# First weight tiles split by hand in halves, one weight tile per unit, and a new sharing of the second layer's split and clamp steps in an attention and two-MLP kernel

## The chip, the cores and the metric

The kernel runs on one core of a Trainium2 chip. The metric is the device time in microseconds (us), from launch to end. The engines are named as in the profile: PE (TensorE, matmuls), PEld (its weight loads), DVE (VectorE), ACT (ScalarE), POOL (GpSimd) and SP (SyncE, which issues DMAs).

## The reference

Banded attention with a slope per head is followed by two MLPs, all on 2304 tokens (4 x 576) of 512 features, 8 heads of 64:

```python
scores = scale * np.matmul(q, k.transpose(0, 1, 3, 2))
rel = pos[:, None] - pos[None, :]
mask = (rel >= 0) & (rel < 128)
scores = np.where(mask, scores + slope * -abs(rel), -1e9)
attn = softmax(scores)                 # over the keys
x = (attn @ v) as [2304, 512]
...
h = np.maximum(x @ w_in, 0.0);  x = h * h @ w_out      # d_ff = 2048
...
h = x @ w_in;  g = h * np.cos(h);  out = g @ w_out
```

## The kernel before, in words

Every matmul with float32 accuracy is done as three matmuls of split operands: each tile is split into a high part (`wh`, `xh`, `rh`/`gh`) that the PE takes as it is, and a low part (`wl`, `xl`, `rl`/`gl`), the rest. ACT makes the high parts (a cast), DVE the low ones (a subtraction).

**Attention.** A step is a pair of heads of 128 query rows, `s` = 4 j + hp. The first 16 steps go as eight pairs (`pairs`) and use "plain" tiles `S0`. For a pair, PE makes scores, DVE the row minima with the bias (`minima`, L666), ACT the exponentials (`exps`, L682), then the rows are scaled by one over their sum (`normalise`, L696 to L706), PE transposes them (L715), ACT copies the transposed tile out of PSUM (L717), POOL masks it with two selects (`transposes`, L722), and PE multiplies with v (`values`, L768). `x_hi` (L788) and `x_lo` (L791) split the result for layer 1. Throughout, `fill(n)` (L123) puts n matmuls on constant data into PE's order, where it would have nothing to do. The first eight pairs and the work up to the second score tile are written out in order by hand under `tc.manual_schedule`; from there a scheduler orders each engine's instructions by the order of the program and by its own estimates, and each engine runs them in that order.

**Layer 1.** `h_mms(i)` (L827 to L829) makes the h tile of a unit i (128 of the 2048 inner columns for 512 tokens), ACT and DVE make the square of its positive part, and `y_mms(i)` (L956 to L958) adds it to y. The raw weight tile `raw_f` of a unit holds both halves, w_in and w_out, and three steps split it: `w_top` (L241, ACT, a copy of the top 16 bits into a zeroed tile `cv`), `w_rest` (L245, DVE, the rest by shift and or), `w_split` (L258, ACT, the high part) and its late step `lo` (L261, DVE, the low part). Each works on 1024 columns. A `tick()` moves each job that is under way by one step and starts new ones ("a": keys and queries or block sums, "w": weights).

**Layer 2.** Its first product is done by seven products of half blocks (`seven`), so that sums of blocks (S1 to S4 of the weights, T1 to T4 of x) have to be formed and split beforehand, and products are put together by copies (L863, L864, L868, L876, ACT) and additions (L865, L871, L874, DVE) into `hs`. Units go in pairs p (`NP` of them), a pair in four quarters with one tick each. Jobs make the weights: `blocks_job(u)` (L348, L364 to L367) and `w2_job(u)` (L295), both with L241 and L245, `x2_sums_job` (L465 and others) the sums of x. `LATE` says at which pair the last two weight blocks may start, `LEAD` after how many ticks a loaded job may. A unit's activation is `cos_reduce` (ACT L905, DVE L906 and L907, a clamp to +-4.7 on DVE, L908, and the absolute value on ACT, L909) and `cos_apply` (the sine on ACT, L917, product on DVE L918, split by L919 and L920). `y_out` copies a block of y (L971) and stores it.

Of the kernel before, what the change touches and what calls it, by code (L numbers as in the profile page):

```python
# [31 lines left out]
INV2PI = 1.0 / (2.0 * math.pi)  # L32
C1 = 6.28125
# [24 lines left out]
START, PLAIN, FILLS = 16, 7, (19, 5, 10, 4, 14, 6)  # L58


A_OPEN, START_W, MERGED = 20, (5,), 16
# [10 lines left out]
NP = NBK * NU  # L72
RING = (2, 3, 4, 5)
# [5 lines left out]
class Job:  # L79


    def __init__(self, key, load, stages, gates=None, source=None, frees=1, ready=None, raws=1):
# [6 lines left out]
def attention_mlp_mlp(ctx: ExitStack, tc: tile.TileContext, kq, s0, v, w1, w2, bias, ident, out):  # L89
# [21 lines left out]
    warm = cst.tile([P, 1], F32, name="warm")  # L111
    dve.memset(halfpi, math.pi / 2)
    act.activation(warm, halfpi, AF.Exp)
# [23 lines left out]
    LATE = (2, 5), (3, 6)  # L137
# [82 lines left out]
    def w_load(layer, f):  # L220
        def load(job):
            job.raw = wp.tile([P, 2048], F32, tag=f"w{f}", name=f"raw_{layer}_{f}")
# [41 lines left out]

    def w_job(layer, f):
# [10 lines left out]
    def w2_job(u):  # L276
# [16 lines left out]
        def lo(job):  # L293
# [4 lines left out]
            ("w2", u), load, [w_top, w_rest, split, lo], {0: aged(u, 1)}, frees=2, ready=lambda: now["y"] >= used(u) and due(u, 1)  # L298
# [12 lines left out]
    def blocks_job(u):  # L311
# [66 lines left out]
        def end(job):  # L378
# [10 lines left out]
            ready=lambda: now["y"] >= used(u) and gp2 is not None and due(u, 0),  # L389
        )  # L390
# [56 lines left out]
    def x2_sums_job(b, k):  # L447
# [33 lines left out]
        def lo(job):  # L481
            for (dst, src), (top, _) in zip(views(job, 1), views(job, 0)):
                dve.tensor_tensor(dst, src, top.bitcast(F32), ALU.subtract)

# [5 lines left out]
        return Job(("x", b, k), load, [sums, hi, lo], {0: gate}, ("y", b), frees=2, raws=2)  # L490

    def x2_job(b, m):
# [6 lines left out]
        def lo(job):  # L499
# [8 lines left out]
            ("y", b),  # L508
        )
# [167 lines left out]
    def exps(steps):  # L677
# [12 lines left out]
        if len(steps) == 2:  # L690
            pool.tensor_scalar(st[:, 2], st[:, 1], 1e-9, None, ALU.add)

    def normalise(*steps):
        st = St.pop(steps)
        if len(steps) == 1:
# [12 lines left out]
    def transposes(*steps):  # L708
# [7 lines left out]
        quick = steps == pairs[-1]  # L716
# [570 lines left out]
```

## Time and profile before

| what | value |
|---|---|
| time, median of 3 runs (lowest to highest) | 903.06 us (902.13 to 904.57) |
| the profiled execution | 904.49 us |
| its span from first to last instruction | 902.8 us (1.7 us lie outside) |
| PE, DVE, ACT, POOL busy | 892.0, 639.4, 531.9, 104.6 us |
| mean granted TensorE clock | 0.998 of full |

The profile's rows come from one profiled execution, whose time stands above the median of the runs by 1.43 us. An engine's idle time counts only where it is on the way to the end; PE is busy for 99% of the span.

### The profile page before, as it was taken

To read this page: it belongs to the slowest core of one execution; us is meant where nothing else is said; L and a number is where in the kernel's file an instruction comes from. 1 tells how busy PE (TensorE), PEld (TensorE's weight loads), DVE (VectorE), ACT (ScalarE), POOL (GpSimd) and SP (SyncE) were. 2 spreads that over 40 slices of the span, in tenths; PEclk is the share of its full clock that TensorE was granted. 3 is DMA by queue.
4 is the path that set the end of the run, shared out by engine and by line. 5 is a ranking of instruction groups with operands and counts; after the bars stand their busy time and mean duration, and the time that the engine had idled before them with its cause. 6 is when DMAs were issued, how large, how long until landed. Compare 5 with 4: busy or idle time off the path is not lost.

```text
span 902.8 us, 15383 instructions
## 1 busy us (share of the span) xinstructions
PE 892.0 (99%) x5474; PEld 764.0 (85%) x5474; DVE 639.4 (71%) x1533; ACT 531.9 (59%) x1177; POOL 104.6 (12%) x164
## 2 busy tenths in 40 slices
PE   9899999999999999999999999999999999999998
PEld 7677788888888888788888889888988989899987
DVE  7699676656676556745776788998877776666654
ACT  6799555455454444524655686776666755655543
POOL 3333221102222112200100100000000000000000
PEclk9999999999999999999999999999999999999999
DMA  9852031311122111224899999977657655655530
GB/s 373 292 219 94 13 128 59 106 47 60 59 71 72 57 48 47 90 97 166 270 313 319 311 344 301 316 224 238 202 179 227 208 168 173 215 182 169 185 127 24
DMA packets 82141, 153.24 MB, mean 170 GB/s; under 512 B 7696, under 2 KB 29584, under 8 KB 82064
## 3 DMA queue, kind: packets, MB, share of 16 engines
q1 hardware_dynamic: 81632, 152.06, 51.0%
q8 instruction: 43, 0.70, 0.3%
q14 instruction: 34, 0.28, 0.1%
q10 hardware_dynamic: 432, 0.20, 0.1%
HBM read 126.01 MB, written 26.21 MB: 169 GB/s over the span
## 4 chain that ended last, share of the span: by engine, by line
PE 83%; DVE 8%; ACT 4%; DMA 3%; issue 1%; POOL 0%; SPq 0%; DVEq 0%; ACTq 0%; POOLq 0%
PE y L956 12%; PE y L957 12%; PE y L958 12%; PE h L827 7%; PE h L829 7%; PE h L828 7%; PE s L855 5%; PE s L857 5%; PE s L856 5%; PE o L768 3%; PE s L616 2%; PE t L715 1%; DVE cv_w L245 1%; DVE w L261 1%; DMA raw_a<-kq_in 1%
## 5 line engine op out<-in xcount | busy, mean ns | idle before, releaser
L956 PE MATMUL y<-rh,w 128*128 128x512 f32 (+1 forms) x320 | 120.9, 379 | 0.0
L827 PE MATMUL h<-xh,w 128*128 128x512 f32 (+1 forms) x320 | 119.7, 374 | 0.0
L957 PE MATMUL y<-rl,w 128*128 128x512 f32 (+1 forms) x320 | 118.6, 371 | 0.0
L958 PE MATMUL y<-rh,w 128*128 128x512 f32 (+1 forms) x320 | 118.5, 370 | 0.0
L828 PE MATMUL h<-xl,w 128*128 128x512 f32 (+1 forms) x320 | 118.1, 369 | 0.0
L829 PE MATMUL h<-xh,w 128*128 128x512 f32 (+1 forms) x320 | 118.0, 369 | 0.0
L956 PE MATMUL y<-gh,w 128*128 128x512 f32 x256 | 101.1, 395 | 0.0
L957 PE MATMUL y<-gl,w 128*128 128x512 f32 x256 | 101.0, 395 | 0.0
L958 PE MATMUL y<-gh,w 128*128 128x512 f32 x256 | 99.7, 389 | 0.0
L883 ACT ACTIVATE a<-h 128x512 f32<-128x512 f32 x72 | 42.9, 596 | 80.1 <-PE h L829 79.9
L722 POOL TENSOR_SCALAR_AFFINE_SELECT p<-p 128x256 f32<-128x256 f32 x104 | 61.6, 593 | 235.0 <-ACT p L717 231.5
L894 DVE TENSOR_TENSOR a<-a 128x512 f32<-128x512 f32 x62 | 43.9, 708 | 48.4 <-ACT rh L893 47.7
L682 ACT ACTIVATE p<-s,st 128x128 f32<-128x128 f32 x112 | 40.1, 363 | 60.2 <-DVE st L666 57.8
L855 PE MATMUL s<-xh,arena 128*128 128x256 f32 x256 | 73.0, 286 | 1.4 <-DVE hs L865 1.2
L857 PE MATMUL s<-xh,arena 128*128 128x256 f32 x256 | 72.4, 283 | 0.0
L856 PE MATMUL s<-xl,arena 128*128 128x256 f32 x256 | 72.3, 283 | 0.0
L827 PEld LDWEIGHTS h<-xh,w 128*128 128x128 f32 x320 | 60.4, 189 | 11.5 <-issue 0.5
L905 ACT ACTIVATE kk<-hs 128x512 int32<-128x512 f32 x64 | 39.6, 631 | 51.6 <-DVE hs L874 50.9
L958 PEld LDWEIGHTS y<-rh,w 128*128 128x128 f32 x320 | 60.3, 188 | 10.4
L829 PEld LDWEIGHTS h<-xh,w 128*128 128x128 f32 x320 | 60.3, 188 | 10.4
L956 PEld LDWEIGHTS y<-rh,w 128*128 128x128 f32 x320 | 60.4, 189 | 9.9 <-issue 1.7
L828 PEld LDWEIGHTS h<-xl,w 128*128 128x128 f32 x320 | 60.4, 189 | 9.3
(142 smaller groups left out, 2207.9 us busy)
## 6 DMA issues: line engine op xcount, KB each, us to landing
arena<-wd SPq DMA_DIRECT2D x256, 256.0 KB, 3.3
raw<-w_in SPq DMA_DIRECT2D x16, 1023.8 KB, 7.9
raw_a<-kq_in SPq DMA_DIRECT2D x44, 256.0 KB, 3.0
raw<-w_in SPq DMA_DIRECT2D x16, 511.8 KB, 7.0
raw_b<-w_in SPq DMA_DIRECT2D x16, 511.8 KB, 6.5
wd<-hi_b SPq DMA_DIRECT2D x10, 512.0 KB, 5.4
v<-v_in SPq DMA_DIRECT2D x18, 256.0 KB, 2.8
y<-ysb SPq DMA_DIRECT2D x18, 256.0 KB, 2.0
```

What stands on the lines that cost most here:

```text
L722: pool.affine_select(pt[:, part], pt[:, part if quick else 0], pattern=[[0, n], [0, 2], [-sign, P]], compare_op=ALU.is_gt if part else ALU ...
L827: te.matmul(o, wh, xh, start=(c == 0 and kt == 0), stop=False, skip_group_check=True)
L828: te.matmul(o, wh, xl, start=False, stop=False, skip_group_check=True)
L829: te.matmul(o, wl, xh, start=False, stop=(kt == KT - 1), skip_group_check=True)
L855: te.matmul(o, wh, xh, start=opens and k == 0, stop=False, skip_group_check=True)
L856: te.matmul(o, wh, xl, start=False, stop=False, skip_group_check=True)
L857: te.matmul(o, wl, xh, start=False, stop=k == 1, skip_group_check=True)
L883: act.activation(Aa[i], Hb.pop(i), AF.Relu)
L894: dve.tensor_tensor(a, a, a, ALU.mult)
L956: te.matmul(o, wh, gh, start=(first and not (two and m % 2)), stop=False, skip_group_check=True)
L957: te.matmul(o, wh, gl, start=False, stop=False, skip_group_check=True)
L958: te.matmul(o, wl, gh, start=False, stop=last, skip_group_check=True)
```

## The change

The core of it, by parts:

- The start: the first two weight tiles, w_0 and w_1, are split in halves of 512 columns each (`w_half_job`; first w_in, then w_out), in steps called by hand (`step`). Raw tiles 0 and 1 use other seats. The last pair is scaled by DVE alone; DVE also makes the small additions of the last two pairs and masks one part of each (`quick`) by a multiplication with `onward`. The fills are changed.
- Layer 1: a new weight job starts in the first tick of a unit, not in each.
- Layer 2: a tick starts at most one step of a job that is marked heavy on DVE (`fits`, `heavy`); the low part of the block sums of x is made in two steps; `LATE` and `LEAD` are lower; and for units NG1 + 6 to NG1 + 17 (pairs 3 to 8) ACT does the clamp.

```diff
-START, PLAIN, FILLS = 16, 7, (19, 5, 10, 4, 14, 6)
-A_OPEN, START_W, MERGED = 20, (5,), 16
+START, PLAIN, FILLS = 16, 7, (19, 5, 10, 4, 14, 4)
+BY_HAND = 2
+ACT_CLIPS = range(NG1 + 6, NG1 + 2 * NU + 2)
...
-    LATE = (2, 5), (3, 6)
+    LATE = (1, 3), (2, 5)
...
     def advance(job):
-        with behind() if timed(job) else ExitStack():
+        with behind() if timed(job) or job.key[0] in ("w", "kq") else ExitStack():
...
     def tick(new="aw", flush=True):
         ticks[0] += 1
+        worked = [0]
+        def fits(job):
+            if now["p"] < 0 or not timed(job) or not job.heavy[job.at]:
+                return True
+            worked[0] += 1
+            return worked[0] == 1
         for job in list(inflight):
-            if job.at not in job.gates or job.gates[job.at]():
+            if (job.at not in job.gates or job.gates[job.at]()) and fits(job):
...
-                if job.raw is None or timed(job) and ticks[0] < job.loaded + (LEAD if now["p"] < 0 else 2 * LEAD - 2):
+                if job.raw is None or timed(job) and ticks[0] < job.loaded + (LEAD + 3 if job.key[0] != "x" and job.key[1] > 5 else LEAD):
                     continue
-                if 0 not in job.gates or job.gates[0]():
+                if (0 not in job.gates or job.gates[0]()) and fits(job):
...
+    def w_half_job(layer, f):
+        def top(job, c):
+            if job.t is None:
+                job.t = cleared.pop(0)
+                w = wp.tile([P, 2048], F32R, tag=f"w{f}", name=f"w_{layer}_{f}")
+                W[layer, f] = (w[:, 0:512], w[:, 1024:1536]), (w[:, 512:1024], w[:, 1536:2048])
+            f16 = job.t.bitcast(F16).rearrange("p (c n two) -> p c n two", c=2, two=2)
+            raw = job.raw.bitcast(BF16).rearrange("p (c n q) -> p c n q", c=2, q=4)
+            act.copy(f16[:, c, :, 1], raw[:, c, :, 2])
+        def half(job, c):
+            return job.t[:, 512 * c : 512 * c + 512]
+        def rest(job, c):
+            raw = job.raw.bitcast(I32).rearrange("p (c n two) -> p c n two", c=2, two=2)
+            t = half(job, c).bitcast(I32)
+            dve.scalar_tensor_tensor(t, raw[:, c, :, 0], 13, t, ALU.logical_shift_right, ALU.bitwise_or)
+        def split(job, c):
+            act.copy(W[layer, f][c][0], half(job, c))
+        def lo(job, c):
+            dve.tensor_tensor(W[layer, f][c][1], half(job, c), W[layer, f][c][0].bitcast(F32), ALU.subtract)
+        steps = [partial(step, c=c) for c in range(2) for step in (top, rest, split, lo)]
+        return Job(("w", layer, f), w_load(layer, f), steps, frees=5)
+    def step(f, times=1):
+        for _ in range(times):
+            advance(queues["w"][f])
...
-        return Job(("x", b, k), load, [sums, hi, lo], {0: gate}, ("y", b), frees=2, raws=2)
+        return Job(("x", b, k), load, steps, {0: gate}, ("y", b), frees=2, raws=2, heavy=(1, 0, 1, 1))
...
-        if len(steps) == 2:
+        if len(steps) == 2 and steps not in pairs[-2:]:
             pool.tensor_scalar(st[:, 2], st[:, 1], 1e-9, None, ALU.add)
...
-                quick = steps == pairs[-1]
-                if len(steps) == 2 and e and (i or quick):
+                if len(steps) == 2 and e and i and steps != pairs[-1]:
                     act.activation(p, p, AF.Copy, scale=r)
...
-        quick = steps == pairs[-1]
+        quick = steps in pairs[-2:]
...
-        dve.tensor_scalar(r, r, -4.7, 4.7, ALU.max, ALU.min)
-        act.activation(r, r, AF.Abs)
+        if i in ACT_CLIPS:
+            act.activation(r, r, AF.Abs)
+            act.activation(r, r, AF.Relu, bias=limit, scale=-1.0)
+        else:
+            dve.tensor_scalar(r, r, -4.7, 4.7, ALU.max, ALU.min)
+            act.activation(r, r, AF.Abs)
...
-        act.activation(r, r, AF.Sin, bias=halfpi, scale=-1.0)
+        if i in ACT_CLIPS:
+            act.activation(r, r, AF.Sin, bias=back, scale=1.0)
+        else:
+            act.activation(r, r, AF.Sin, bias=halfpi, scale=-1.0)
...
-            for k in range(len(pairs)):
+            for k in range(len(pairs) - 1):
...
-                tick("aw" if k in START_W else "a")
+                tick("a")
+                if k == 5:
+                    step(0)
+            exps(pairs[-1])
+            step(1)
+            values_of_block(FILLS[4])
+            x_hi(LAST - 1)
+            normalise(*pairs[-1])
+            step(0)
+            x_lo(LAST - 1)
+            transposes(*pairs[-2])
+            fill(2)
             transposes(*pairs[-1])
+            step(0, 2)
+            step(1)
+            fill(FILLS[3])
             scores((START,))
             fill(FILLS[5])
             for a in pairs[-2]:
                 values(a)
-            tick("w")
             fill(FILLS[3])
...
-            tick("aw" if s >= STEPS else "a")
+            tick()
...
-            tick()
+            tick("aw" if s >= STEPS else "a")
```

How this moves DVE's instructions is shown at three places, before and after; line numbers of after are higher by some 55 to 65 for the same work (L761 is L706 of before, L846 is L791, L774 is L719). First, DVE at the last two pairs: `s_6` and `s_0` are the tiles of the second-last and the last pair, `cv_0` and `cv_1` the work tiles of w_0 and w_1. Before:

```order
L245 SCALAR_TENSOR_TENSOR cv_0_150<-raw_0_180,cv_0_150 128x1024
L591 TENSOR_SCALAR bias_sb<-base_sb 128x256
L697 RECIPROCAL st_501<-st_501 128x4
L706 TENSOR_SCALAR s_0_118<-s_0_118,st_501 128x128 x2
L791 TENSOR_TENSOR xl_115<-o_540,xh_114 128x4x128
L261 TENSOR_TENSOR w_0_536<-cv_0_150,w_0_536 128x1024
L719 TENSOR_TENSOR s_0_118<-t_589,onward 128x512
```

And after:

```order
L761 TENSOR_SCALAR s_6_128<-s_6_128,st_443 128x128 x3
L752 TENSOR_SCALAR st_506<-st_506 128x4
L753 RECIPROCAL st_506<-st_506 128x4
L761 TENSOR_SCALAR s_0_122<-s_0_122,st_506 128x128 x4
L302 SCALAR_TENSOR_TENSOR cv_0_154<-raw_0_184,cv_0_154 128x512
L846 TENSOR_TENSOR xl_119<-o_540,xh_118 128x4x128
L774 TENSOR_TENSOR s_6_128<-t_582,onward 128x512
L774 TENSOR_TENSOR s_0_122<-t_592,onward 128x512
L308 TENSOR_TENSOR w_0_502<-cv_0_154,w_0_502 128x512
```

The step on all of w_0 stood ahead of the last pair's scaling; now half of it stands behind four scalings.

Second, DVE in layer 2 at the weight tile of u = 6 (`cv_w_6`), where a quarter begins (`hs_0` the first half of a unit pair). Before:

```order
L907 SCALAR_TENSOR_TENSOR r_6279<-kk_6278,r_6279 128x512
L245 SCALAR_TENSOR_TENSOR cv_w_6_6269<-raw_6_6014,cv_w_6_6269 128x1024
L908 TENSOR_SCALAR r_6279<-r_6279 128x512
L865 TENSOR_TENSOR hs_0_6302<-hs_0_6302,s_0_6300 128x256
L907 SCALAR_TENSOR_TENSOR r_6334<-kk_6333,r_6334 128x512
L295 TENSOR_TENSOR w_6_6331<-cv_w_6_6269,w_6_6331 128x1024
```

And after:

```order
L964 SCALAR_TENSOR_TENSOR r_6069<-kk_6068,r_6069 128x512
L922 TENSOR_TENSOR hs_0_6077<-hs_0_6077,s_0_6075 128x256
L264 SCALAR_TENSOR_TENSOR cv_w_6_6059<-raw_6_5807,cv_w_6_6059 128x1024
L964 SCALAR_TENSOR_TENSOR r_6111<-kk_6110,r_6111 128x512
L518 TENSOR_TENSOR t_0_6132<-raw_a_0_4956 128x256
```

The addition L865 (now L922) has passed the weight step, and no clamp stands between.

Third, DVE where y of block 1 is copied out (`ysb_1_1`, `ysb_1_3`) in layer 2. Before:

```order
L871 TENSOR_TENSOR hs_1_7497<-hs_1_7497,s_0_7494 128x256
L971 COPY ysb_1_1_7587<-y_1_6700 128x512
L874 TENSOR_TENSOR hs_0_7496<-hs_0_7496,s_1_7495 128x256
...
L908 TENSOR_SCALAR r_7610<-r_7610 128x512
L971 COPY ysb_1_3_7593<-y_3_6702 128x512
L920 TENSOR_TENSOR gl_7604<-r_7526,gh_7603 128x512
L865 TENSOR_TENSOR hs_0_7618<-hs_0_7618,s_0_7616 128x256
```

And after:

```order
L928 TENSOR_TENSOR hs_1_7513<-hs_1_7513,s_0_7510 128x256
L518 TENSOR_TENSOR t_1_7580<-raw_a_0_7445 128x256
L520 TENSOR_TENSOR t_1_7580<-raw_a_1_7446,raw_a_0_7445 128x256
L519 TENSOR_TENSOR t_1_7580<-raw_a_1_7446,t_1_7580 128x256
L1035 COPY ysb_1_1_7608<-y_1_6728 128x512
...
L1035 COPY ysb_1_3_7614<-y_3_6730 128x512
L984 TENSOR_TENSOR gl_7629<-r_7542,gh_7628 128x512
L969 TENSOR_SCALAR r_7635<-r_7635 128x512
L922 TENSOR_TENSOR hs_0_7643<-hs_0_7643,s_0_7641 128x256
```

Three sums of x have moved ahead of the first copy, and the clamp has moved from ahead of the second copy to right ahead of the addition.

## Rows read from the trace of the kernel before

**Rows 1.** Busy time, share and instructions by engine, from the page.

```profile
PE 892.0 (99%) x5474; PEld 764.0 (85%) x5474; DVE 639.4 (71%) x1533; ACT 531.9 (59%) x1177; POOL 104.6 (12%) x164
```

**Rows 2.** Waits of PE: releaser, total us, times, longest us.

```profile
PE s L855 <- DVE hs L865: 1.2, 2, 0.8
...
PE t L715 <- DVE p L706: 1.0, 2, 0.6
PE t L715 <- ACT p L682: 0.7, 2, 0.5
```

**Rows 3.** Windows of 20 us: length, busy us by engine, clock, DMA.

```profile
60.00:80.00 20.00, 20.00 (x126) 15.30 (x125) 19.46 (x44) 19.23 (x36) 7.34 (x11) 1.00 0.25 86
80.00:100.00 20.00, 19.40 (x119) 14.71 (x118) 18.46 (x45) 17.58 (x34) 7.18 (x11) 1.00 0.17 59
...
140.00:160.00 20.00, 19.40 (x118) 16.00 (x117) 14.07 (x42) 9.08 (x30) 3.98 (x8) 1.00 0.20 67
...
520.00:540.00 20.00, 20.00 (x133) 18.15 (x131) 17.08 (x34) 16.31 (x31) 0.00 (x0) 1.00 0.97 344
...
580.00:600.00 20.00, 19.89 (x122) 16.95 (x121) 18.48 (x35) 15.33 (x28) 0.00 (x0) 1.00 0.74 253
```

**Rows 4.** The same view in two stretches of the start: PE, PEld, DVE, ACT, POOL.

```profile
28.50:33.40 4.90, 2.65 (x27) 1.84 (x26) 4.10 (x9) 3.71 (x12) 2.35 (x4) 1.00 0.72 260
33.40:36.80 3.40, 3.40 (x24) 2.52 (x26) 1.40 (x2) 1.83 (x2) 2.78 (x3) 0.50 1.01 420
```

**Rows 5.** Timeline of PE: start us, us, instruction, idle before and releaser.

```profile
29.20 1.09 PE L768 MATMUL o<-s,v 128*64 128x128 f32 x16 [0.68 <-POOL s L722]
...
31.29 0.30 PE L715 MATMUL t<-id_sb,s 128*128 128x128 f32 x1 [0.41 <-DVE s L706]
32.77 0.62 PE L715 MATMUL t<-id_sb,s 128*128 128x128 f32 x3 [1.17 <-ACT s L704]
...
38.88 0.50 PE L827 MATMUL h<-xh,w 128*128 128x512 f32 x1
```

**Rows 6.** Timeline of DVE around the last two pairs.

```profile
23.87 0.68 DVE L706 TENSOR_SCALAR s<-s,st 128x128 f32<-128x128 f32 x3
...
27.54 0.18 DVE L697 RECIPROCAL st<-st 128x4 f32<-128x4 f32 x1 [0.64 <-POOL st L691]
27.82 1.41 DVE L706 TENSOR_SCALAR s<-s,st 128x128 f32<-128x128 f32 x3
29.15 1.21 DVE L245 SCALAR_TENSOR_TENSOR cv<-raw,cv 128x1024 int32<-128x1024 int32 x1
...
32.56 1.63 DVE L261 TENSOR_TENSOR w<-cv,w 128x1024 fp32r<-128x1024 f32 x1
```

**Rows 7.** Timeline of POOL around the last two pairs.

```profile
22.88 0.22 POOL L691 TENSOR_SCALAR st<-st 128x4 f32<-128x4 f32 x1 [1.44 <-DVE st L666]
...
27.75 1.41 POOL L722 TENSOR_SCALAR_AFFINE_SELECT s<-s 128x512 f32<-128x512 f32 x2 [0.24 <-ACT s L717]
29.69 0.85 POOL L691 TENSOR_SCALAR st<-st 128x4 f32<-128x4 f32 x1 [0.54 <-ACT s L682]
32.48 2.80 POOL L722 TENSOR_SCALAR_AFFINE_SELECT s<-s 128x512 f32<-128x512 f32 x3 [1.95 <-ACT s L717]
```

**Rows 8.** Timeline of ACT at the last pair's scaling.

```profile
32.30 0.70 ACT L704 ACTIVATE s<-s,st 128x128 f32<-128x128 f32 x2
```

**Rows 9.** Groups by line in layer 2 (DVE 500 to 620, ACT 520 to 580): busy, mean, idle before.

```profile
L908 DVE TENSOR_SCALAR r<-r 128x512 f32<-128x512 f32 x20 | 8.4, 422 | 0.1
...
L917 ACT ACTIVATE r<-r,halfpi 128x512 f32<-128x512 f32 x11 | 8.0, 726 | 0.2
...
L863 ACT COPY hs<-s 128x256 f32<-128x256 f32 x6 | 2.2, 371 | 2.4 <-PE s L857 2.4
```

**Rows 10.** Timeline of DVE at two places in layer 2.

```profile
579.38 1.22 DVE L245 SCALAR_TENSOR_TENSOR cv_w<-raw,cv_w 128x1024 int32<-128x1024 int32 x1
...
696.44 0.69 DVE L971 COPY ysb<-y 128x512 f32<-128x512 f32 x1 [1.21 <-DMA out<-ysb]
```

More of the change, by code (lines that the diff above doesn't have):

```diff
@@ L1 @@
 import math
+from functools import partial
 from contextlib import ExitStack
@@ L32 @@
 INV2PI = 1.0 / (2.0 * math.pi)
+CLIP = 4.6875
 C1 = 6.28125
@@ L79, with __init__ @@
 class Job:
-    def __init__(self, key, load, stages, gates=None, source=None, frees=1, ready=None, raws=1):
+    def __init__(self, key, load, stages, gates=None, source=None, frees=1, ready=None, raws=1, heavy=None):
+        self.heavy = heavy
         self.key, self.load, self.stages, self.frees, self.raws = key, load, stages, frees, raws
@@ L111, in attention_mlp_mlp @@
     warm = cst.tile([P, 1], F32, name="warm")
+    limit = cst.tile([P, 1], F32, name="limit")
+    back = cst.tile([P, 1], F32, name="back")
     dve.memset(halfpi, math.pi / 2)
+    pool.memset(limit, CLIP)
+    pool.memset(back, math.pi / 2 - CLIP)
     act.activation(warm, halfpi, AF.Exp)
@@ L221, in load @@
         def load(job):
-            job.raw = wp.tile([P, 2048], F32, tag=f"w{f}", name=f"raw_{layer}_{f}")
+            seat = f if f >= BY_HAND else SEAT - 1 - f
+            job.raw = wp.tile([P, 2048], F32, tag=f"w{seat}", name=f"raw_{layer}_{f}")
             sp.dma_start(job.raw.bitcast(U16)[:, 0:4095], (w1, w2)[layer][f][:, 1:4096])
@@ L297, in w2_job @@
         return Job(
-            ("w2", u), load, [w_top, w_rest, split, lo], {0: aged(u, 1)}, frees=2, ready=lambda: now["y"] >= used(u) and due(u, 1)
+            ("w2", u), load, [w_top, w_rest, split, lo], {0: aged(u, 1)}, frees=2, ready=lambda: now["y"] >= used(u) and due(u, 1), heavy=(0, 1, 0, 1)
         )
@@ L389, in blocks_job @@
             ready=lambda: now["y"] >= used(u) and gp2 is not None and due(u, 0),
+            heavy=(0, 1, 1, 1, 1, 0),
         )
@@ L479, in hi, with lo @@
                 act.copy(dst, src)
-        def lo(job):
-            for (dst, src), (top, _) in zip(views(job, 1), views(job, 0)):
+        def lo(job, which):
+            for (dst, src), (top, _) in list(zip(views(job, 1), views(job, 0)))[which]:
                 dve.tensor_tensor(dst, src, top.bitcast(F32), ALU.subtract)
+        steps = [sums, hi, partial(lo, which=slice(0, 2)), partial(lo, which=slice(2, 4))]
         def gate():
@@ L508, in x2_job @@
             ("y", b),
+            heavy=(0, 1),
         )
@@ L694, in normalise @@
         st = St.pop(steps)
-        if len(steps) == 1:
+        if len(steps) == 1 or steps in pairs[-2:]:
             dve.tensor_scalar(st[:, 2], st[:, 1], 1e-9, None, ALU.add)
@@ L811, in h_mms @@
             for f in fs:
-                run_until(("w", layer, f))
+                if f >= BY_HAND:
+                    run_until(("w", layer, f))
+                assert f >= BY_HAND or queues["w"][f].at >= 4
         now["h"] = i
@@ L1007, in attention_mlp_mlp @@
     queues["a"] += [x2_job(NBK, m) for m in range(2)]
-    queues["w"] += [w_job(0, f) for f in range(NF)]
+    queues["w"] += [w_half_job(0, f) for f in range(BY_HAND)] + [w_job(0, f) for f in range(BY_HAND, NF)]
+    started["w"] = BY_HAND
     for u in range(NU - 2):
@@ L1071, in attention_mlp_mlp @@
             minima(pairs[0])
-            for k in range(len(pairs)):
+            for k in range(len(pairs) - 1):
                 j = k // 2 - 1
-                if k + 1 < len(pairs):
-                    minima(pairs[k + 1])
+                minima(pairs[k + 1])
                 make_bias(1, (k,))
                 exps(pairs[k])
-                final = k + 1 == len(pairs)
-                if final:
-                    tick("", False)
                 if k % 2 and j >= 0:
-                    values_of_block(FILLS[4] if final else 0)
+                    values_of_block()
                     x_hi(j)
                 if k:
-                    fill(0 if final else FILLS[3])
+                    fill(FILLS[3])
                     transposes(*pairs[k - 1])
@@ L1091, in attention_mlp_mlp @@
                     x_lo(j)
-                tick("aw" if k in START_W else "a")
+                tick("a")
[10 more added lines that the diff above has]
+            fill(2)
             transposes(*pairs[-1])
+            step(0, 2)
+            step(1)
+            fill(FILLS[3])
             scores((START,))
@@ L1097, in attention_mlp_mlp @@
                 values(a)
-            tick("w")
             fill(FILLS[3])
-            for k in range(2):
-                hps = slice(2 * k, 2 * k + 2)
-                if k:
-                    for a in pairs[-1]:
-                        values(a)
-                x_hi(LAST, hps)
-                x_lo(LAST, hps)
-                tick("")
+            x_hi(LAST, slice(0, 2))
+            step(0)
+            x_lo(LAST, slice(0, 2))
+            for a in pairs[-1]:
+                values(a)
+            x_hi(LAST, slice(2, 4))
+            step(0)
+            x_lo(LAST, slice(2, 4))
             waiting.clear()
+            step(1, 2)
             minima((START,))
+            step(0, 2)
+            make_bias(1, (H - 1,))
+            inflight.append(queues["w"][1])
             tick("a")
```

1 line of the change is left out of this document (added).

## Prediction

> **What bounds the kernel now.** I read the page's busy times first: TensorE (PE) is busy 892.0 of 902.8 us [rows 1]. No engine can shorten the run except by taking away one of PE's own idle stretches, or a stretch in which PE works at the half clock. So I looked for those. The waits of PE [rows 2] name only a few, and the windows show where PE is short of its full 20 us: 0.60 at 80 to 100, 0.60 at 140 to 160, 0.11 at 580 to 600 and much more at the start [rows 3, 4]. The start is worst: from 28.50 to 33.40 PE is busy 2.65 of 4.90 us, and in the 3.40 us behind that, in which it is busy throughout, its granted clock is 0.50, the lower of its two levels [rows 4]. Everything else in the program is already full of matmuls.
>
> **The start, removed.** PE's timeline shows three waits ahead of that stretch: 0.68 on a POOL select, 0.41 on DVE's scaling and 1.17 on ACT's scaling of the last pair, whose transposes end at 33.39 (32.77 + 0.62) [rows 5]. Why is the scaling late? On DVE [rows 6] the whole-tile step on w_0 (L245, 1.21) stands between the two scalings, and the last pair's reciprocal waits for POOL's little add L691, which took 0.85 where it usually takes 0.22 [rows 7]. ACT's share, two instructions from 32.30 to 33.00, comes last of all [rows 8], behind the 1024-wide copy of w_0.
>
> In after, DVE does both adds itself, so the 0.64 that DVE waited for POOL ahead of the reciprocal [rows 6] falls away too. I walk it: three scalings end at 29.23 - 0.64 = 28.6; add and reciprocal about 0.4 (two instructions of 0.2; the reciprocal is 0.18 [rows 6]); four scalings at most 1.2 (three took 1.41 beside POOL's selects [rows 6, 7], four without them are 1.2 at 0.3 each). So the last pair is scaled by about 30.2 and transposed by 31.05, where it was 33.39: **2.3 us sooner**. The half steps of w_0 (estimated 0.65 each, half of 1.21) now stand behind these, where PE waits for none of them before its first h matmul.
>
> From those transposes to the first h matmul at 38.88 [rows 5] before took 5.5 us, 3.4 of it at the half clock. What PE does there at the full clock is one set of scores 0.65, two sets of value matmuls of 1.03 and three short fills of 0.48: 4.05 us. The selects behind the last pair's transposes are two instead of three (2.80 for three [rows 7]), so they are ready by 32.6, ahead of the values. So h(0) starts at 35.1: another **1.4 to 1.5 sooner**, if the clock does not fall. I think it does not, since the three waits that came before it (0.68, 0.41, 1.17) are gone or short.
>
> **The start, added.** Nothing is for free: w_2, whose whole-tile steps now follow closer behind the hand-made halves, should have its lower part late for h(2) by about 0.7 (its DVE steps are 1.21 and 1.63 long [rows 6], and PE comes 3.8 sooner). The next scores' normalise stands behind these, which makes a wait of about 0.85 where the transposes waited up to 0.6 [rows 2]. I keep 3.4 us of the 3.8 as the gain when PE has done h(3). Bounds: 1.9 (the low clock stays) to 4.5 (no late w_2).
>
> **What the port costs.** Beside POOL's two selects (27.75, 1.41 long) three DVE scalings took 1.41, where three at 23.87 took 0.68; and POOL's add beside L245 took 0.85 and not 0.22 [rows 6, 7]. So one of the two stands still while the other runs. After has more DVE work beside the last selects (multiplies by `onward`, half steps). Before's two selects were not longer for it: 0.70 each with DVE busy beside them, against 0.93 each for the three later [rows 7]. I take 0.3 from the gain, between 0 and two half steps of 0.65, because only one half step stands beside each select. The Trainium skill ("SBUF — State Buffer", section "SBUF: two separate sides") says that VectorE and GpSimd share a port pair under an exclusive lock and that the loser blocks for the whole instruction. By that rule a half step that begins first would delay each of the two selects by its whole length, 1.3 in all, and the sum would be 1.0 longer; the rows for the add agree with it, and those for the selects show only DVE as the loser.
>
> **Layer 1.** The swapped ticks make one weight tile a unit, where several were made close together. DVE's total is not changed: it was 19.46 busy of 20 in 60 to 80 and 18.46 in 80 to 100, with ACT at 19.23 and 17.58 [rows 3]. By counting the instructions of one unit in the order of after at the durations of the trace, DVE has 5.1 us of work up to unit 9 and 6.1 after that, against PE's 6.6 to 7.1. So the weights keep a margin of 1.3 us or more, and the waits before the weights and the `p` tiles at 80 to 100 (0.60) and at 140 to 160 (0.60) [rows 2, 3] should go: **-1.2** (between -1.7, with the remaining ones at the end of layer 1, and 0, if DVE's order brings the same waits elsewhere).
>
> **Layer 2.** Three edits act on DVE and ACT, and PE is full: 20.00 of 20 at 520 to 540, 19.89 at 580 to 600 [rows 3]. One heavy DVE step a tick takes L245 (579.38, 1.22 [rows 10]) from in front of L865: worth the 0.11 at 580 to 600 [rows 3] that PE shows as idle and up to 0.3 more that matmul starts lost behind it, so -0.3 to -0.4. The clamp costs DVE 0.42 each [rows 9]. Twelve of them go to ACT, where each is a Relu with a bias tile, as long as the Sin with its bias, 0.73 [rows 9]: 12 x 0.73 = 8.8 us of ACT work, none of it PE's, since ACT is at 16.31 of 20 before the change [rows 3] and PE's product copies there, L863, have ACT waiting for PE (2.4 us in six [rows 9]) and not the reverse. It hides; if the cover fails, each product copy is late by at most 0.73. Against that: the block sums of x in the last blocks now stand in DVE's order ahead of the copy of y (L971) that DVE makes at the end of block 1, which waited 1.21 on its output DMA with gl and L865 queued behind [rows 10] and gave one of PE's two waits on L865, 0.8 [rows 2]. Three sums of 0.42 ahead of it are mostly inside that 1.21; but the clamp is now ahead of L865 (0.42), and the tile that is copied comes later. I take +0.8 for it (0 to 1.3). Together **+0.4** for layer 2 (-0.5 to +1.5).
>
> **Sum.** -3.4 + 0.3 - 1.2 + 0.4 = -3.9 on the profiled execution, 904.49 to 900.6. That execution lies 1.43 above the median of the runs, 903.06, so on the median the forecast is 903.06 - 3.9 = **899.2 us**. A measurement of this kernel tells about 0.3%, 2.7 us, from no change: faster means below 900.4.
>
> **Rivals.**
> - *The low clock stays* (chance 0.2). The fills are fewer (six to four before the values), and PE has waits of its own ahead of them still. Then 1.5 of the 3.4 is missing: 899.2 + 1.5 = 900.7. For it: in the trace of before the half clock follows a stretch with PE 54% busy [rows 4]; against it: three waits fewer.
> - *Clips fill ACT* (chance 0.12). ACT at 16.31 of 20 [rows 3] gets 0.73 twice a pair, 1.8 pairs in 20 us, 2.6 more: 18.9 of 20, if none of ACT's work moved away. If the product copies come 0.3 to 0.5 late in each of six pairs: +1.8 to +3, so about 901.5.
> - *Weights just in time are late* (chance 0.07), the one that ends slower. Place: layer 1, units 2 to 15, where a tile is now finished only one unit ahead. It decides from the point where DVE's unit (6.1) plus waits behind ACT passes PE's (6.6): then PE waits for each w's lower part. 0.5 x 14 = 7 us, less the start's 3.1 and with layer 2's 0.4: 903.06 + 7 - 3.1 + 0.4 = 907.4. For it: DVE at 97% at 60 to 80. Against: that window holds the pile that is now spread.
> - *The start gives nothing* (chance 0.08): a half step of w_0 or w_1 is late for y(0) or h(1), and PE stands there as long as it did at 31 to 33. Then 903.06 - 1.2 + 0.4 = 902.3.
>
> **How the numbers follow.** The forecast's own case has 0.53 (its range 897.3 to 900.4 from the bounds of its terms). Of it 0.51 is faster and 0.02 the same. The low clock splits 0.09 faster, 0.11 same; ACT 0.02 and 0.10; the start without gain is 0.08 same; late weights 0.07 slower. That is faster 0.62, same 0.31, slower 0.07. The range for 8 in 10 goes from 896.6 (layer 1 at -1.7, no late w_2, layer 2 at -0.5) to 902.4, which leaves out the late weights and some of the start without gain.
>
> **What would show it.** Right: h(0) at about 35 with a granted clock of 1.00 throughout, h(3) done about 3.4 sooner, no idle PE at 80 and 150, no L245 right ahead of L865, about 8.8 us more of ACT. Wrong: a half-clock stretch again, PE waits on w tiles in layer 1 (each new line of the waits with `w` as releaser), or PE waits on the product copies of pairs 3 to 8.

## The result and the profile after

The changed kernel takes 908.20 us (median of 6 runs, 907.32 to 910.65), the kernel before 903.64 us (6 runs): a ratio of 1.0054 with a 95% interval of 1.0037 to 1.0070. It is slower by 4.6 us where 3.9 us (4.4 against these runs) were to be won. The profiled execution took 907.66 us, with a span of 905.6.

Where the time went is seen best by the moment at which PE reaches the same work in both traces. The table has the start of the first h matmul of a unit (the last two lines: the first and one of the last products of layer 2), in us from the span's start, and the difference of each kernel to the profile of before. The last five columns belong to experiments below. Each column is one profiled execution; the profile of before has the half clock at its start [rows 4].

| work | before | changed | keys free | start only | keys behind, on before | before again | layer 2 only |
|---|---|---|---|---|---|---|---|
| h(0) | 38.9 | -3.72 | -3.47 | -3.57 | -0.05 | -2.40 | +0.29 |
| h(4) | 63.2 | -3.30 | -2.76 | -1.28 | -0.11 | -2.46 | +0.28 |
| h(8) | 92.8 | -3.99 | -2.92 | +1.48 | -1.02 | -2.42 | +0.28 |
| h(12) | 121.0 | -4.47 | -2.93 | +1.47 | -1.48 | -2.41 | +0.31 |
| h(16) | 151.9 | +0.97 | -2.39 | +1.55 | +3.60 | -2.19 | +0.31 |
| h(32) | 263.5 | +2.32 | -2.31 | +1.50 | +4.92 | -2.22 | +0.32 |
| first of layer 2 | 507.0 | +2.99 | -2.28 | +1.40 | +5.82 | -2.26 | +0.22 |
| near the end | 879.7 | +2.79 | -1.95 | +1.56 | +5.35 | -2.72 | -0.95 |

So the changed kernel has its 3.7 us at the start and still holds 4.5 at h(12). Then 5.4 us are lost between 121 and 152 us, another 2.0 up to layer 2, and layer 2 changes next to nothing.

The start came as forecast. PE's timeline of the changed kernel has no wait where before had three [rows 5], and h(0) starts at 35.16:

```profile
28.68 1.09 PE L823 MATMUL o<-s,v 128*64 128x128 f32 x16
29.70 0.66 PE L770 MATMUL t<-id_sb,s 128*128 128x128 f32 x4
...
30.41 0.60 PE L770 MATMUL t<-id_sb,s 128*128 128x128 f32 x4
...
35.16 0.51 PE L884 MATMUL h<-xh,w 128*128 128x512 f32 x1
```

The windows of the same two stretches as in [rows 4] (length, then PE, PEld, DVE, ACT and POOL busy, the granted clock, DMA) show PE full, with fills where nothing else is ready, and its clock at 1.00 throughout:

```profile
28.50:33.40 4.90, 4.83 (x59) 3.93 (x58) 4.34 (x13) 3.58 (x9) 1.40 (x3) 1.00 0.94 353
33.40:36.80 3.40, 3.40 (x33) 2.54 (x30) 2.82 (x6) 2.57 (x6) 0.00 (x0) 1.00 0.67 242
```

DVE there, against [rows 6], and POOL's two selects, against [rows 7]:

```profile
27.31 1.40 DVE L761 TENSOR_SCALAR s<-s,st 128x128 f32<-128x128 f32 x3
...
29.61 0.87 DVE L761 TENSOR_SCALAR s<-s,st 128x128 f32<-128x128 f32 x4
30.40 0.68 DVE L302 SCALAR_TENSOR_TENSOR cv<-raw,cv 128x512 int32<-128x512 int32 x1
...
31.60 1.28 DVE L774 TENSOR_TENSOR s<-t,onward 128x512 f32<-128x512 f32 x2
```

```profile
27.22 1.40 POOL L777 TENSOR_SCALAR_AFFINE_SELECT s<-s 128x512 f32<-128x512 f32 x2 [1.39 <-ACT s L772]
31.05 1.29 POOL L777 TENSOR_SCALAR_AFFINE_SELECT s<-s 128x512 f32<-128x512 f32 x2 [2.43 <-ACT s L772]
```

The loss is in the waits of PE (releaser, total us, times, longest). Against [rows 2] there are new ones: a copy of transposed scores, 2.3 at once, the keys' low part, 0.8, and the wait for scaled scores, 2.3 in all where it was 1.0:

```profile
PE t L770 <- DVE p L761: 2.3, 3, 1.1
PE t L770 <- ACT p L772: 2.3, 1, 2.3
PE s L912 <- DVE hs L922: 1.5, 1, 1.5
...
PE s L672 <- DVE KS L603: 0.8, 1, 0.8
```

and in the windows of layer 1, where PE falls to 17.03 of 20 at 140 to 160, where it had 19.40 before [rows 3]. DVE is full just ahead of that, 17.91 at 120 to 140 (16.34 before):

```profile
120.00:140.00 20.00, 19.48 (x116) 15.51 (x115) 17.91 (x42) 12.73 (x34) 4.08 (x7) 1.00 0.25 78
140.00:160.00 20.00, 17.03 (x104) 13.49 (x103) 14.36 (x45) 8.78 (x29) 3.83 (x9) 1.00 0.19 62
```

The chain of work in that stretch (start us, us, what) shows what goes round there. A pass begins with the low part of the square (`rl`), goes to the low parts of keys and queries (`KS`, `ql`), which free their raw tile, then to the load of the next raw tile, its copies on ACT, the exponentials, the scaling, the square, and the low part again:

```profile
124.87 0.68 DVE rl L952
125.58 0.42 DVE KS L603
126.04 0.43 DVE ql L604
126.53 2.96 DMA raw_a<-kq_in
...
129.82 0.40 ACT qh L599
...
130.72 0.70 ACT p L738 x4
131.45 0.70 DVE st L752
...
133.03 0.61 DVE a L951
...
134.39 0.42 DVE KS L603
134.82 0.43 DVE ql L604
135.31 2.96 DMA raw_a<-kq_in
```

From load to load on this chain that is 135.31 - 126.53 = 8.8 us. The edit in `advance` puts this order there: with `behind` for key and query jobs ("kq"), their subtractions stand on DVE behind the latest low part of a square. The experiments show whether it makes the loss.

### The profile page after: what moved, and what is told of

Read it like the earlier page. It is cut to its first block, busy times and chain, and to the rows that moved or that the text cites. A ratio compares the mean times of both kernels' runs of the same rounds, so it can differ in the third digit from the quotient of the medians.

```text
span 905.6 us, 15397 instructions
## 1 busy us (share of the span) xinstructions
PE 891.8 (98%) x5478; PEld 764.1 (84%) x5478; DVE 641.2 (71%) x1530; ACT 539.0 (60%) x1191; POOL 100.3 (11%) x163
## 4 chain that ended last, share of the span: by engine, by line
PE 84%; DVE 7%; ACT 4%; DMA 3%; issue 1%; POOL 0%; DVEq 0%; ACTq 0%; SPq 0%; POOLq 0%
PE y L1020 13%; PE y L1021 12%; PE y L1022 12%; PE h L884 7%; PE h L885 7%; PE h L886 7%; PE s L912 6%; PE s L913 6%; PE s L914 6%; PE o L823 3%; PE s L672 2%; DMA raw_a<-kq_in 2%; PE t L770 1%; ACT p L738 1%; DMA out<-ysb 1%
## 5 line engine op out<-in xcount | busy, mean ns | idle before, releaser
L1020 PE MATMUL y<-rh,w 128*128 128x512 f32 (+1 forms) x320 | 121.0, 379 | 0.0
L1020 PE MATMUL y<-gh,w 128*128 128x512 f32 x256 | 101.2, 395 | 0.0
L738 ACT ACTIVATE p<-s,st 128x128 f32<-128x128 f32 x112 | 40.0, 362 | 58.4 <-DVE st L722 54.9
L1020 PEld LDWEIGHTS y<-rh,w 128*128 128x128 f32 x320 | 60.6, 189 | 10.0 <-issue 1.7
```

The source lines that it names most:

```text
L738: act.activation(Pt[steps][:, 1, i, e], Sc[a][e][:, own(j)], AF.Exp, bias=st[:, 0, i, e : e + 1], scale=-1.0, accum_out=st[:, 1, i, e : e ...
L1020: te.matmul(o, wh, gh, start=(first and not (two and m % 2)), stop=False, skip_group_check=True)
```

## The experiments

Theory A was that the weight splits, spread at one tile per unit, meet the key and query splits, and that DVE is too full. By the starts of their last step (L280), five of the sixteen tiles are finished from 106 to 138 us; before, fourteen were finished by 98 us, and two stood at 123 and 129. Theory B was the order `behind` for key and query jobs. Each ratio is against the runs of the kernel before that shared the chip, whose medians were 903.54, 903.87, 902.81 and 903.69 us in the four sets.

**The ticks put back.**

```diff
-            tick()
+            tick("aw" if s >= STEPS else "a")
...
-            tick("aw" if s >= STEPS else "a")
+            tick()
```

> The changed kernel with the two ticks of a unit in layer 1 put back, so that weight jobs start in the second. Theory A (one weight tile per unit lets the last weight splits run until 138 us, into the stretch in which the key and query splits begin, and DVE at over 90% there delays the chain): the 5.5 us lost between 121 and 152 us come back, about 903 us or below. Theory B (the key and query jobs, now ordered behind the unit's square, close a loop through their own DMA of one pass per unit): little back, 907 to 908.5.

Measured 909.34 us, ratio 1.0061 (1.0046 to 1.0077). Nothing comes back. But the edit does not undo the spreading: the last steps of the weights run until 147 us here. So the run shows that the ticks do not spread the weights, and theory A's full DVE is left to the runs below.

**No order behind the square for weights, keys and queries.**

```diff
-        with behind() if timed(job) or job.key[0] in ("w", "kq") else ExitStack():
+        with behind() if timed(job) or job.key[0] in () else ExitStack():
```

> The changed kernel with the order behind the square taken away from both the first layer's weight jobs and the key and query jobs, as before the change. Theory A: no more than 1 us back, 907 to 908.5. Theory B: the loop from the low split over the next DMA of raw_a to the exponentials gets shorter by the 1.4 us of the two square steps on DVE, and 4 to 5 us come back, 903 to 904.

Measured 905.26 us, ratio 1.0025 (1.0011 to 1.0039): 2.9 us below the changed kernel, between the two theories. The trace has fourteen weight tiles finished by 97 us again, and the last two at 124 and 129, with the new ticks. So it is the order behind the square that spreads them, not the ticks. But there is a new loss earlier: h(8) is 0.65 later than before. The waits of PE name ACT's exponentials:

```profile
PE t L770 <- ACT p L738: 2.9, 3, 1.6
```

and ACT's timeline shows what stands ahead of these exponentials (L738): copies of keys that wait for their load, and weight copies:

```profile
78.92 0.41 ACT L598 CAST KS<-raw_a 128x256 fp32r<-128x256 f32 x1 [0.81 <-DMA raw_a<-kq_in]
...
79.54 1.36 ACT L260 CAST cv_w<-raw 128x1024 f16<-128x1024 bf16 x1
80.76 0.36 ACT L738 ACTIVATE p<-s,st 128x128 f32<-128x128 f32 x1
```

**Keys and queries free, weights still behind the square.**

```diff
-        with behind() if timed(job) or job.key[0] in ("w", "kq") else ExitStack():
+        with behind() if timed(job) or job.key[0] in ("w",) else ExitStack():
```

> The changed kernel with that order taken away from the key and query jobs alone; weight jobs keep it. Theory B: the same as with both taken away, 903 to 904. Theory A: 907 to 908.5. If it lies between the two, the order of the weight jobs has a part of its own.

Measured 902.83 us, ratio 0.9997 (0.9985 to 1.0009): 5.4 us below the changed kernel, as theory B said. The 5.4 lost between h(12) and h(16) become 0.5, and the wait of 2.3 on L772 is gone. What ACT waits for between 120 and 150 us tells it apart. Changed kernel:

```profile
ACT p L738 <- DVE st L722: 3.5, 1, 3.5
ACT KS L598 <- DMA raw_a<-kq_in: 2.6, 4, 0.8
```

With the keys free:

```profile
ACT p L738 <- DVE st L722: 7.1, 4, 2.4
ACT KS L598 <- DMA raw_a<-kq_in: 0.8, 2, 0.7
```

ACT waits longer on DVE there, but for the keys' loads 0.8 instead of 2.6. And DVE is as full with weights as in the changed kernel (17.9 and 18.2 of 20 from 120 to 140), so the rest of theory A, a full DVE, does not make the loss by itself. The DVE rows of the same kernel show the subtraction ahead of the square's low part now, where the chain above had it behind:

```profile
131.09 0.93 DVE L951 TENSOR_TENSOR a<-a 128x512 f32<-128x512 f32 x1 [0.40 <-ACT rh L950]
132.05 0.42 DVE L603 TENSOR_TENSOR KS<-raw_a,KS 64x256 fp32r<-64x256 f32 x1
132.51 0.69 DVE L952 TENSOR_TENSOR rl<-a,rh 128x512 fp32r<-128x512 f32 x1
```

The traces show a second effect of that order, which the chain does not: the keys lose their lead. The loads into the raw tiles of keys and queries (`raw_a`), counted from the first, start at (us):

| kernel | third | eighth | ninth | eleventh |
|---|---|---|---|---|
| before | 56.3 | 78.4 | 122.9 | 136.8 |
| keys free | 54.0 | 72.7 | 119.6 | 135.0 |
| changed | 95.2 | 126.5 | 129.8 | 138.0 |
| keys behind on DVE, on before (below) | 98.8 | 130.9 | 132.7 | 140.8 |
| keys behind on ACT alone (below) | 90.6 | 119.6 | 126.8 | 135.5 |

There are two raw tiles, so the third to the eighth load start as the first six tiles have been split. Without the order that is done by 79 us. With it on DVE it falls between 95 and 131 us, up to and into the stretch where PE then waits.

**The start alone.** The ticks, the order and all of layer 2 as before (`LATE`, `LEAD`, no `fits`, no clamps on ACT, the low part in one step); only the start is changed.

> Only the start of the change (halves by hand, last pair on DVE, quick masks, fills); ticks, order behind the square, and all of layer 2 as before. Both theories: h(0) at about 35.2 us and the 3.7 us kept to the end, 899.5 to 900.5. If the gain is given back in layer 1 here too, neither theory holds: then a sooner start meets the same supply of keys and queries, and the time is 902 to 904.

Measured 906.39 us, ratio 1.0049 (1.0030 to 1.0068). A miss: neither theory holds the gain here. PE has 3.57 us at h(0) and has lost 5.05 at h(8), by the same waits as without any order: 3.4 us for ACT's exponentials, in four places. ACT waited between 45 and 95 us:

```profile
ACT KS L598 <- DMA raw_a<-kq_in: 2.8, 3, 1.6
ACT cv_w L260 <- POOL cv_w L250: 2.1, 3, 1.1
```

So a sooner start alone runs into ACT's queue: key copies that wait for their loads, and weight copies, some of which wait for POOL to clear their work tile, stand ahead of the exponentials. With the weight jobs behind the square and the new ticks 4.4 us of it are kept (h(8) at -2.92 there, +1.48 here). The order by itself keeps 3.6, by the trace without any order and with the new ticks (h(8) at +0.65).

**Which engine's order.**

```diff
-        with behind() if timed(job) or job.key[0] in ("w", "kq") else ExitStack():
+        with behind() if timed(job) or job.key[0] == "w" else behind("act") if job.key[0] == "kq" else ExitStack():
```

> The changed kernel, with the key and query jobs ordered behind the unit's square on ACT alone; their subtractions on DVE are free as before. If the loss comes from the subtraction of keys and queries behind the square's subtraction on DVE, which frees the raw tile late and so starts the next load of 2.96 us late: about as with these jobs wholly free, 902 to 903.5. If the copies on ACT behind the square make it: about as the changed kernel, 907 to 908.5.

Measured 903.41 us, ratio 0.9999 (0.9986 to 1.0011). And `behind("dve")` in its place:

> The mirror of it: key and query jobs behind the square on DVE alone, free on ACT. By the DVE account 906.5 to 908.5; by the ACT account 902 to 903.5. If both halves lie between, each order has a share.

Measured 910.34 us, ratio 1.0074 (1.0061 to 1.0087). So the order on DVE makes the loss, as far as the medians tell. PE then waits 1.7 for the keys' low part (L603) and 2.3 on L772 again. The time is above the 908.5 that was expected at most, and this profile has 3.4 us at the half clock from 148.1, inside the stretch of the loss. The order on ACT alone is not quite free in its trace: there 2.65 are lost between h(12) and h(16) (-4.06 to -1.41), of a lead that had grown by 1.1 more at h(8) than with the keys free, and layer 2 starts at -1.46 against -2.28. Its loads are late too (the table above), yet the eighth starts at 119.6 and not at 126.5. So late loads alone do not make the whole loss.

**That order by itself, on the kernel before.**

```diff
-        with behind() if timed(job) else ExitStack():
+        with behind("dve") if job.key[0] == "kq" else behind() if timed(job) else ExitStack():
```

> The kernel before with one edit: key and query jobs ordered behind the unit's square on DVE. If the order closes a loop through the raw tiles' loads by itself: 3 to 5 us slower, 906.5 to 908.5, with the loss between 120 and 165 us. If it costs only while weight splits are still made there, as one tile per unit does, then 903.5 to 904.5, since here they end at 98 us.

Measured 907.35 us, ratio 1.0055 (1.0041 to 1.0069): one edit of the change is as slow as the whole change, and it is so with fourteen weight tiles finished early and only two left for this stretch. The loss lies at the same places: 5.1 us between h(12) and h(16) in the table, then about 1 at 261 and 1 at 380 us. The lead of the keys is lost by this edit too: ACT copies the first tile at 51.2 in both, but DVE's subtraction of it comes at 98.2, right behind a square's low part, and not at 55.7. Before, and with the edit:

```profile
55.68 0.56 DVE L529 TENSOR_TENSOR KS<-raw_a,KS 64x256 fp32r<-64x256 f32 x1
```

```profile
97.52 0.69 DVE L895 TENSOR_TENSOR rl<-a,rh 128x512 fp32r<-128x512 f32 x1 [0.71 <-ACT rh L891]
98.23 0.42 DVE L529 TENSOR_TENSOR KS<-raw_a,KS 64x256 fp32r<-64x256 f32 x1
```

The profiled execution was the slowest of the six (909.84), so its column stands higher than the median. The waits of PE in it:

```profile
PE t L715 <- DVE p L706: 4.0, 4, 1.8
PE s L616 <- DVE KS L547: 1.5, 1, 1.5
```

**Keys free, old ticks.** As with the keys free, and the ticks put back as in the first experiment.

> Key and query jobs free, weight jobs behind the square, and the two ticks of a unit as before the change. The swap of the ticks alone is then read against the same kernel with the new ticks (902.8). If one weight tile per unit in the first tick is worth what the changed kernel kept over the old ticks (1.1 us): 903.5 to 904.5. The forecast's own account of layer 1, by which spreading takes away two waits: 904. If the order behind the square does it all: 902.8.

Measured 906.68 us, ratio 1.0040 (1.0025 to 1.0055): 3.9 us over the same kernel with the new ticks, more than was expected. Its profile is of the slowest of six executions (909.72) and does not show the ticks alone. From h(1) to h(4) it loses 5.2 us (-3.45 to +1.79), where the kernel with the new ticks loses 0.7. 2.3 of it is one wait on the cast of the square (PE y L1020 for ACT rh L948). From 48.2 this execution has 3.4 us at the half clock, which costs some 1.7 (an estimate: half of it):

```profile
48.00:50.00 2.00, 2.00 (x7) 1.21 (x5) 1.55 (x2) 1.02 (x7) 0.95 (x1) 0.55 1.02 430
```

Four of the six had a mean granted clock of 1.000, and these took 905.9 to 906.8, so the median stands. With the weights behind the square the new ticks are worth about 3.9; what they are worth without that order no pair of runs isolates.

**The weights' part alone**, on the kernel before: new ticks, weight jobs behind the square, nothing else.

> The kernel before with one part of the change: the ticks of layer 1 swapped and its weight jobs ordered behind the unit's square; key and query jobs free, start and layer 2 as before. If the order of the weight jobs is what keeps the start's gain in the changed kernel and is worth something by itself: the waits at 81 and 88 us (0.9 us in all) go, about 902. If it only helps where PE comes sooner: 903, no change. If weights come late with the whole-tile start: 904 or more.

Measured 904.18 us, ratio 1.0001 (0.9989 to 1.0014): no gain by itself. In its trace layer 2 even starts 0.95 later than before (+0.17 at h(0)). What it does is keep a sooner start.

**Layer 2.** The layer-2 part alone, on the kernel before:

> The kernel before with the layer-2 part alone (one heavy step per tick, the lower LEAD and LATE, 12 clamps on ACT). The prediction's account: 0.4 us slower. From the profiles of the changed kernel: 0.2 to 0.3 either way, 902.5 to 903.5. If the clamps fill ACT: 904.5 or more.

Measured 904.39 us, ratio 1.0002 (0.9991 to 1.0014). Keys free and all of layer 2 as before:

> Start and layer 1 of the change with the key and query jobs free, and all of layer 2 as before. From the profiles, the changed layer 2 loses 0.65 at the end of block 1 and 0.3 in pairs 0 to 4, and wins 0.85 around u = 6: the sum is 0.3 lost with the keys free, so this should be 902.5 (902 to 903.5 by noise). If layer 2's edits do gain, it is 903.5 or more. As the version that may beat both, it should be below the kernel before by 1 us.

Measured 903.63 us, ratio 1.0009 (0.9996 to 1.0021): not the 902.5 that was expected, and not below the kernel before. Keys free and no clamps on ACT (`ACT_CLIPS = ()`):

> As the run with the keys and queries free, but with the clamp on DVE everywhere (no clamp on ACT). If ACT's 12 clamps cost nothing because they hide: 902.8. If they delay product copies (the rival of the prediction, 1.8 to 3 us): 900 to 901. If they are what wins around u = 6: 903.5.

Measured 904.09 us, ratio 1.0018 (1.0005 to 1.0031). Keys free and the block sums of x again eight ticks after their load:

```diff
-                ... job.loaded + (LEAD + 3 if job.key[0] != "x" and job.key[1] > 5 else LEAD):
+                ... job.loaded + (LEAD + 3 if job.key[0] == "x" or job.key[1] > 5 else LEAD):
```

> Key and query jobs free, and the block sums of x in layer 2 start 8 ticks after their load again and not 5. If their three sums ahead of the copy of y on DVE make the wait of 1.5 us on the product's addition at the end of block 1: that wait falls to about 0.75, as in the kernel before, and the time to about 902.0. If the clamp moved ahead of that addition makes it: no change, 902.8.

Measured 903.16 us, ratio 1.0002 (0.9991 to 1.0012). Layer 2 is worth nothing that can be measured, in either direction; the clamps on ACT, if anything, help by about 1 us beside the one heavy step (without them PE has a new wait of 0.7 on the addition L928), but the intervals with and without them overlap. The wait of PE at the end of block 1, 0.75 before and 1.49 in the changed kernel, is made by the sums ahead of the copy in part at most. With the sums later it falls from 1.44 (keys free) to 0.94. But with layer 2 as before it is 1.36, though DVE's order is the old one there: its copy still waits 1.82 us for its store, where the kernel before had 1.21 [rows 10]. And with the layer-2 part alone there is no wait at that place at all. So it comes with the new start:

```profile
694.90 0.69 DVE L1035 COPY ysb<-y 128x512 f32<-128x512 f32 x1 [1.82 <-DMA out<-ysb]
```

**The kernel before, profiled again.**

> The kernel before once more, for a second profile. If the half-clock stretch at the start is not in each run, this one may show the start at the full clock: then h(0) starts about 1.5 us sooner than 38.88 and the span is about 901. If the stretch is there again: 38.9 and 902 to 903.

Measured 901.76 us, span 900.0. This execution went from 28.5 us to h(0) at the full clock, and yet it has the three waits that the prediction took for the cause of the half clock:

```profile
28.35 1.09 PE L768 MATMUL o<-s,v 128*64 128x128 f32 x16 [0.66 <-POOL s L722]
...
30.43 0.30 PE L715 MATMUL t<-id_sb,s 128*128 128x128 f32 x1 [0.40 <-DVE s L706]
31.91 0.62 PE L715 MATMUL t<-id_sb,s 128*128 128x128 f32 x3 [1.18 <-ACT s L704]
...
36.48 0.50 PE L827 MATMUL h<-xh,w 128*128 128x512 f32 x1
```

```profile
33.40:36.80 3.40, 3.40 (x42) 2.54 (x41) 1.90 (x3) 1.58 (x3) 1.92 (x3) 1.00 0.97 405
```

h(0) starts at 36.48 and not at 38.88, 2.4 sooner where 1.5 was expected. But 0.85 of it was there long before: the value matmuls start at 28.35 and not at 29.20 [rows 5], and PE is already ahead by as much at 6 us, since the nineteen fills at the start of the program took 4.24 us in the first profile and 3.74 here:

```profile
1.16 4.24 PE L123 MATMUL junk<-idle 128*128 128x256 bf16 x19 [1.16 <-POOL idle L118]
1.16 3.74 PE L123 MATMUL junk<-idle 128*128 128x256 bf16 x19 [1.16 <-POOL idle L118]
```

They took 4.24 in the changed kernel too. So the half clock is 1.55 of the 2.4, and with the same first 6 us the new start is worth 36.48 + 0.85 - 35.16 = 2.2 us against an execution at the full clock.

No kernel here beats the kernel before beyond its interval; the one with the keys free is the best of the changed ones, and equal to it.

## Why the prediction was wrong

**The step that failed** is the account of layer 1: -1.2 us, from "one weight tile a unit" with DVE's total unchanged. It took each engine's work per unit against PE's, and it priced the swapped ticks and the weights alone. It gave no price to the key and query jobs that the same edit of `advance` puts behind the square. That order adds no instruction to any engine. It takes the keys' lead away, 40 to 50 us for the third to eighth load, and it lengthens a chain that crosses engines and a DMA: the raw tile comes free only behind the square's low part, and the next load of 2.96 us, ACT's copies and the next scores follow from there. From h(4), where the forecast counts the start as done, to layer 2 the term was +6.3 (-3.30 to +2.99). The order of the keys makes 5.3 us at layer 2: that is the difference between +2.99 and -2.28 with the keys free. It is 5.4 between the medians, and 4.5 when the order is put on the kernel before by itself, on DVE alone. That this order is the cause is shown by these runs; how the loss divides between the late loads and the longer pass is not, since no run changes one without the other.

The weights' part of the same term did not come either. With the keys free, h(4) to layer 2 is +0.5 (-2.76 to -2.28) and not -1.2, and by itself on the kernel before it gains nothing. The forecast's own figures gave it less room than it said: 6.1 us of DVE's work against PE's 6.6 leave 0.5, not 1.3 or more.

**Who spreads the weights** was wrong too: with the new ticks alone, fourteen tiles are finished by 97 us as before; the order behind the square moves the last five to between 106 and 138 us.

**The start** was right in its trace, to a tenth: the last transposes ended at 31.01 (31.05 forecast), h(0) at 35.16 (35.1 forecast). Its two parts were right too, by the second profile of before: 2.2 for the waits (2.3 forecast) and 1.5 for the clock (1.4 to 1.5). Some of that tenth is luck. DVE waited 0.49 for ACT's exponentials ahead of the last scalings, which the forecast did not have, and then took 0.87 for the four where it had allowed 1.2. And the terms behind the transposes (0.65, twice 1.03, three times 0.48) add up to 4.15, not 4.05; 4.15 is what was measured.

The reason given for the half clock, three waits, is not shown: the same waits were there in an execution at the full clock, so they are not enough to bring it. It does not come in each execution: 32 of 98 runs of the kernel before had a mean granted clock of 0.999 or more, with a median of 901.9 us, against 904.0 for the other 66. (In the profiles a mean below 0.999 always goes with a stretch of 3.4 us at the half clock.) With the new start it is rarer, as the forecast took it: 75 of 107 runs of kernels that have it reach 0.999, against 43 of 128 without it, and none of eleven profiles has the half clock at the start, against four of five.

What failed here is that the gain was taken as kept after h(3). Alone it is lost again by h(8).

**The port** was priced at 0.3; it cost nothing that shows. The two selects took 1.29, and no half step ran beside them: one ended at 31.08, as the first select began, and the next began at 32.79, behind both, and what DVE did in between reads one of its inputs from PSUM. So the worry was not put to the test. The three scalings beside the first selects were longer (1.40, against 0.87 for four). The Trainium skill ("SBUF — State Buffer", section "SBUF: two separate sides") has the loser of the shared port blocked for a whole instruction; the trace agrees for these scalings. For the selects, the forecast read from the kernel before that only DVE loses. The mean of 0.93 that it used hides one select that lost there, beside the step L261 that had begun at 32.56 and took 1.63; the other two took 0.64 and 0.63:

```profile
33.19 1.50 POOL L722 TENSOR_SCALAR_AFFINE_SELECT s<-s 128x512 f32<-128x512 f32 x1
```

**Layer 2** was +0.4, and is -0.2 in the trace (+2.99 to +2.79), less than the same program moves there between its two profiles (-2.26 to -2.72). By itself it is no change (1.0002). The weight step is out of the way of the addition, as said: L922 now stands at 582.15 and L264 at 582.48.

```profile
582.15 0.41 DVE L922 TENSOR_TENSOR hs<-hs,s 128x256 f32<-128x256 f32 x1
582.48 1.22 DVE L264 SCALAR_TENSOR_TENSOR cv_w<-raw,cv_w 128x1024 int32<-128x1024 int32 x1
```

The clamps cost ACT what was said, 0.725 each beside the values of [rows 9], and hide:

```profile
L967 ACT ACTIVATE r<-r,limit 128x512 f32<-128x512 f32 x6 | 4.4, 725 | 0.1
```

The end of block 1 came out worse by about 0.7, near the 0.8 forecast, but not for the reason given: the layer-2 part alone has no wait there.

**The rivals.** The one that ended slower (late weights, 0.07) had the place right, layer 1, and its 907.4 came near 908.2, but by luck: in the changed kernel none of PE's listed waits is for a weight tile. The others (ACT full, low clock, no gain at the start) did not happen either.

**What stays open.** Why the copy at the end of block 1 waits longer for its store with the new start (1.40 to 2.17 us in eleven profiles, 1.21 or less in the others); what makes the half clock come in one execution and not in another; and how much of the loss is the load itself and how much the late start of the loads. A third raw tile would bear on that; no run tried it.

## What to carry to other kernels

An edit that only reorders can cost more than one that adds work: follow what the moved instruction frees (here a raw tile, whose next load of 3 us is then on the chain) and how far ahead its job could run before, not only what its engine has left per unit. Price every kind of job that an edit's condition names, also those that the description of the change does not speak of. And a gain at the start is a gain only if the queues behind it are ready for PE sooner: read what stands ahead of the first critical instructions in each in-order queue before counting it as kept.

## What the runs showed of the hardware that was not expected

The same program, with waits of the same length (0.66, 0.40 and 1.18 against 0.68, 0.41 and 1.17 us), was granted 0.50 of the TensorE clock, the lower of its two levels, for 3.4 us at its start in one execution and 1.00 in another. The last value matmuls and fills from the last transposes to h(0) took 5.49 us in the one (33.39 to 38.88) and 3.95 in the other (32.53 to 36.48).
